# A hash attention and gated feed-forward kernel on one core: operand placement, a transfer's queue, the order of early loads, and the last output chunk

## The chip, the core and the metric

The kernel runs on one NeuronCore of a Trainium2 chip. The metric is the device time of one execution in microseconds (us); the figure given for a kernel is the median of its timed runs. Five engines work side by side, each on its own list of instructions in order: TensorE (PE in the profile, its weight loads PEld), VectorE (DVE), ScalarE (ACT), GpSimd (POOL) and SyncE (SP), which here only issues transfers. Transfers (DMAs) can be issued from SP's, ScalarE's or GpSimd's list; the issuing instruction first waits for what it needs, and holds up what is behind it on that list.

## The reference

The first part is attention in which a query sees only keys with the same hash. For each of 4 x 8 heads, with 768 positions of 64 values:

```python
q_bits = (np.einsum('bhsd,dk->bhsk', q, proj) > 0)      # 6 bits each; k_bits likewise
mask = q_bucket[:, :, :, None] == k_bucket[:, :, None, :]
scores = np.where(mask, scale * np.matmul(q, k.transpose(0, 1, 3, 2)), -1000000000.0)
attn = softmax(scores)                                   # over the keys
x = (attn @ v) rearranged to (3072 tokens, 512)
```

The second part is a gated feed-forward block with weights of 512 x 1536, 512 x 1536 and 1536 x 512, given in double precision:

```python
g = x @ w_gate;  silu = g / (1.0 + np.exp(-g))
out = (silu * (x @ w_val)) @ w_out                       # (3072, 512), float32
```

## The kernel before, in words

**Memory.** Tiles come from pools that are laid out in the order in which they are opened (L69 to L76): `wordp` (three buffers of 4096 bytes a partition, raw weight words), `stagep` (two of 12288 bytes, weights being prepared), `small` (three buffers each of the tiles `e`, 4 bytes, and `few`, 48 bytes), then `xparts_p`, `lastp`, the weight ring and the pools of the two parts.

**Attention.** The heads are taken two at a time: 16 pairs, each with two halves of 384 queries and six chunks of 128 keys, so 12 units a pair. For a pair:

- `front` prepares it. For pair 0, TensorE transposes q and k (`transpose`, L418, "tps") and `hash_own` (L455) multiplies by the projection ("hps"), takes signs on ScalarE (L441) and spreads them to the second head's rows with VectorE (`spread_k` L447, the copy at L463). The blocks are done one by one by `prepare_pair`, called before the units and within the first of them (L501, L614). For later pairs VectorE transposes k and q (L474), and `hash_next` (L465) does both hashes at once; here q's signs are copied to the second head's rows by a transfer, `spread_q` (L452, "qb<-qb"), which SP's list issues.
- `score(u)` (L494) multiplies k and q ("sc" from "qT,kT"), then adds the product of the sign rows ("sc" from "qb,kb"), which acts as the mask, and ScalarE takes exponentials into the tile `A` (L507). VectorE adds up the weights (L539, L543, L546).
- `attend(u)` (L510) multiplies the weights with v ("av").
- `total` (L551) and `invert` (L565) send the sums through small transfers on SP's list ("few<-row", "sums<-few", "r<-sums"), and `norm` divides.

The loop over pairs (L605) runs all 12 units' scores, then the hash of the next pair, then all 12 `attend`s. `load(n + 2, ...)` fetches later pairs on SP's list: q and k (eight transfers of 96 KB, L337) and v (L316). q and k have one buffer each, so their loads wait until the pair before has been transposed. At the start SP's list holds pair 0's loads, `load_words(2)` (two of 512 KB, L126), and then pair 1's q, k and v; GpSimd's list has the third words (L409 to L412).

**Weight pieces.** Between these steps (`begin_pieces`, `advance_pieces`, L170 to L184) ScalarE and VectorE turn the 36 weight pieces from double precision into three float32r parts (L135 to L164). GpSimd's list stores them to DRAM ("ram<-stage") and fetches the next words.

**The gated block.** The tokens come in three blocks of 1024. The x of a block is four tiles, one for each pair of heads, of 2 x 3 x 512 values: three parts, of which the first two are multiplied with the weights' first two parts ("a") and the third with the third ("n"); the difference corrects the rounding. `x_home` (L250) chooses the tile: block 0 has all four in `xparts_p`, block 1 its first two in `stagep`, and block 2 its last two in `stagep`. The matmuls are in `up` (L672): for a gate or value step, 16 of "a" and 8 of "n", with weights from a ring that GpSimd refills (L244). The down steps ("D" in `order`, "o" in the profile) take three hidden tiles at a time; the last of a block adds eight chunks of 128 tokens into the output tiles. In the very last step each chunk has nine matmuls into a tile of two PSUM banks: three of the correction, then six of the main product; `end` (L756) subtracts the one (L760), adds the other (L768), and SP's list stores the chunk (L775).

Of the kernel before, what the change touches and what calls it, by code (L numbers as in the profile page):

```python
# [13 lines left out]
ALU = mybir.AluOpType  # L14
# [5 lines left out]
def kernel(  # L20
# [20 lines left out]
    nc = tc.nc  # L41
# [25 lines left out]
    TOWARD = 1 - 2.0**-13  # L67

    konst = ctx.enter_context(tc.tile_pool(name="konst", bufs=1))  # L69
    wordp = ctx.enter_context(tc.tile_pool(name="wordp", bufs=3))  # L70
    stagep = ctx.enter_context(tc.tile_pool(name="stagep", bufs=2))
    small = ctx.enter_context(tc.tile_pool(name="small", bufs=3))
    xparts_p = ctx.enter_context(tc.tile_pool(name="xparts", bufs=1))
    lastp = ctx.enter_context(tc.tile_pool(name="lastp", bufs=1))
    RINGS = (3, 3)
# [43 lines left out]
    def load_words(count, queue=None):  # L119
        queue = queue or queues[0]  # L120
        for i in range(len(words), min(count, NPIECE)):
            words[i] = t = wordp.tile([P, PIECE, 2], I32, tag="words", name="words")
            to = t.rearrange("p f w -> p (f w)")
            if len(pieces[i].shape) == 3:
                to = to.rearrange("p (j c) -> p j c", j=NJ)
            queue.dma_start(to, pieces[i])  # L126
# [171 lines left out]
    def attention(scope):  # L298
# [13 lines left out]
        def fetch(n, name, queue, half=None):  # L312
            b, pr = pairs[n]
            if name == "v":
                t = raws["v", n] = raw.tile([P, 2, NCH, D], FP32, tag="vraw", name="vraw")
                queue.dma_start(  # L316
                    t.rearrange("p h c d -> p h (c d)"),
                    v[b, 2 * pr : 2 * pr + 2].rearrange("h (p c) d -> p h (c d)", c=NCH),
                )
                return  # L320
            src = q if name == "q" else k
            if not half:
                raws[name, n] = raw.tile([P, NCH, 2, D], FP32, tag=name + "raw", name=name + "raw",
                                         bufs=1)
            t = raws[name, n]
            if n == 0:
                cs = slice(None) if half is None else slice(half * CH, (half + 1) * CH)
                for h in range(2):
                    queue.dma_start(t[:, cs, h, :],
                                    src[b, 2 * pr + h].rearrange("(p c) d -> p c d", c=NCH)[:, cs, :])  # L330
                return
            blocks = t.rearrange("p c a b -> p (c a b)").rearrange(
                "p (c a d) -> p c a d", a=P // BLOCK, d=BLOCK)
            for h in range(2):
                for x in range(D // BLOCK):
                    at = h * D + x * BLOCK
                    queue.dma_start(  # L337
                        blocks[at : at + BLOCK],
                        src[b, 2 * pr + h][:, x * BLOCK : (x + 1) * BLOCK].rearrange(
                            "(a p c) d -> p c a d", c=NCH, p=BLOCK))  # L340
# [65 lines left out]
        for t in (sides["k", 0], sides["q", 0], sides["q", 1]):  # L406
            nc.gpsimd.memset(t, 0.0)

        load_words(2, nc.sync)  # L409
        for name, queue in (("q", nc.sync), ("k", nc.sync), ("v", nc.sync)):  # L410
            fetch(1, name, queue)
        load_words(3)  # L412

        T = {}
        bits = {}
# [1 line left out]
        def front(n):  # L417
            def transpose(name, half):  # L418
                if (name, n) not in T:
                    T[name, n] = opnd.tile([P, S], FP32, tag=name + "T", name=name + "T")  # L420
                ps = bank("tps")
                for i in range(CH):
                    nc.tensor.transpose(ps[:, i * P : (i + 1) * P],
                                        raws[name, n][:, half * CH + i, :, :].rearrange("p h d -> p (h d)"),
                                        ident)
                nc.scalar.activation(T[name, n][:, half * HQ : (half + 1) * HQ], ps[:, 0:HQ], AF.Copy,
                                     scale=2 / OFF if name == "k" else 1.0)

            bits["q", n] = sides["q", n % 2]
            bits["k", n] = sides["k", n % 2]  # L430
            low, high = slice(0, BLOCK), slice(D, D + BLOCK)

            def hash_blocks(todo):
                tile_ = bank("hps")
                for i, (name, half) in enumerate(todo):
                    nc.tensor.matmul(tile_[i * BLOCK : (i + 1) * BLOCK, 0:HQ], hash_w,  # L436
                                     T[name, n][:, half * HQ : (half + 1) * HQ],
                                     start=True, stop=True)

                def sign(i, name, half, to=low, **how):  # L440
                    nc.scalar.activation(bits[name, n][to, half * HQ : (half + 1) * HQ],  # L441
                                         tile_[i * BLOCK : (i + 1) * BLOCK, 0:HQ], AF.Sign,
                                         **(how or {"bias": nudge[name]}))

                return [lambda i=i, at=at, **how: sign(i, *at, **how) for i, at in enumerate(todo)]

            def spread_k(times, cols=slice(0, S)):  # L447
                b = bits["k", n][:, cols]
                for to, by in ((high, times[1]), (low, times[0])):
                    nc.vector.tensor_scalar(b[to], b[low], scalar1=by, scalar2=None, op0=ALU.mult)  # L450

            def spread_q():  # L452
                nc.sync.dma_start(bits["q", n][high], bits["q", n][low])

            def hash_own(*todo):  # L455
                for f in hash_blocks(todo):
                    f()
                for name, half in todo:
                    cols = slice(half * HQ, (half + 1) * HQ)
                    if name == "k":  # L460
                        spread_k(mask, cols)
                    else:
                        nc.vector.tensor_copy(bits["q", n][high, cols], bits["q", n][low, cols])  # L463

            def hash_next(todo):  # L465
                q0, q1, *ks = hash_blocks(todo)
                q0()
                q1()
                spread_q()
                return ks + [lambda: spread_k(times_k)]  # L470

            def transpose_blocks(name):
                T[name, n] = opnd.tile([P, S], FP32, tag=name + "T", name=name + "T")
                nc.vector.transpose(T[name, n], raws[name, n].rearrange("p c h d -> p (c h d)"))  # L474

            order = [("q", 0), ("q", 1), ("k", 0), ("k", 1)]
            if n:
                return [lambda name=name: transpose_blocks(name) for name in "kq"] + [
                    lambda: hash_next(order)]
            turns = [lambda x=x: transpose(*x) for x in order]  # L480
            return [turns[2], turns[0], lambda: hash_own(("k", 0)), lambda: hash_own(("q", 0)),
                    turns[3], turns[1], lambda: hash_own(("k", 1), ("q", 1))]

        units = [(n, half, c) for n in range(len(pairs)) for half in range(2) for c in range(NCH)]
        acc = {}
# [8 lines left out]
        def score(u):  # L494
            n, half, c = units[u]
            qs = slice(half * HQ, (half + 1) * HQ)
            ks = slice(c * P, (c + 1) * P)
            sc = [bank("sc")[:, 0:HQ] for _ in range(2)]
            for x, start in ((T, True), (bits, False)):
                if u < 2 and not start:  # L500
                    prepare_pair(1)  # L501
                for h in range(2):
                    rows = slice(h * D, (h + 1) * D)
                    nc.tensor.matmul(sc[h], x["k", n][rows, ks], x["q", n][rows, qs],  # L504
                                     start=start, stop=not start)
            for h in range(2):
                nc.scalar.activation(weights(u)[:, h, 0:HQ], sc[h], AF.Exp,  # L507
                                     scale=SCALE * (OFF / 2 if n == 0 else 1.0))
# [84 lines left out]
        def prepare_pair(count):  # L593
            for _ in range(count):
                if steps:
                    rest.extend(f for f in steps.pop(0)() or [] if f)
# [56 lines left out]
    def gated_block(scope):  # L653
# [7 lines left out]
        def two_banks(name):  # L661
            return pp.tile([P, 2, 512], FP32, tag="pp", name=name)
# [35 lines left out]
        def atoms_of(kind, n):  # L698
# [33 lines left out]
            else:  # L732
# [47 lines left out]
                ahead = 4 if part == NF // NQ - 1 else 0  # L780
                for c in range(ahead):
                    yield lambda c=c: start(c, range(NQ - 1))
                for c in range(NCB):
                    def chunk(c=c):
                        start(c, [NQ - 1] if c < ahead else range(NQ))
                        end(c)
                    yield chunk
# [96 lines left out]
```

## Time and profile before

| | |
|---|---|
| three timed runs | 923.06, 923.29, 925.82 us |
| median | 923.29 us |
| the profiled execution | 927.82 us |
| its span, first to last instruction | 926.0 us |
| granted TensorE clock, mean | 0.998 |
| TensorE busy | 912.7 us (99%) |
| VectorE, ScalarE, GpSimd busy | 666.4 (72%), 456.2 (49%), 91.6 us (10%) |

Attention takes the first third of the span, the gated block the rest. Matmuls are pipelined, so a busy TensorE row says only that nothing was missing there; how long a stretch of matmuls takes is read from their starts, in the chain of waits and in tables of stages. A line of a timeline gives the start, the duration, the engine, the line of the kernel, the operation, its output and inputs by the program's names, and how many there were; a bracket gives the idle time before it, and what ended it. A "q" behind an engine's name (SPq) means its list of issued transfers.

### The profile page before, as it was taken

Reading aid. Unit: us, or ns where it says so; the run is one execution under the profiler, and the core shown is the slowest. Engines: PE = TensorE matmul, PEld = TensorE weight load, DVE = VectorE, ACT = ScalarE, POOL = GpSimd, SP = SyncE. Lnnn points to the kernel's source line nnn. Section 1 sums busy time; section 2 is a strip of 40 time slices with the busy share of each in tenths; the row PEclk is TensorE's granted clock in tenths of the full one; section 3 lists DMA queues with packets and bytes.
Section 4 is the critical chain, followed back from the end, with each engine's and each line's share of the span. In section 5 each row is a group of like instructions: output and inputs, shape, how many; then the busy total and the mean of one; then the engine's idle time right before and its main releaser. Section 6 shows DMA issues by size and latency. Waiting matters only on the chain.

```text
span 926.0 us, 12980 instructions
## 1 busy us (share of the span) xinstructions
PE 912.7 (99%) x4789; PEld 638.9 (69%) x4789; DVE 666.4 (72%) x768; ACT 456.2 (49%) x814; POOL 91.6 (10%) x182
## 2 busy tenths in 40 slices
PE   8999989999999999999999999999999999999997
PEld 3444544444444478888888788888887888888886
DVE  4889989889989858779786756464658754474746
ACT  6889868888888654452414133331313233313220
POOL 2011100001101111000100000101010100001000
PEclk9999999999999999999999999999999999999999
DMA  7678787767886599685756563434444642526232
GB/s 171 136 185 205 201 207 172 166 180 200 242 213 206 179 384 318 229 284 206 292 187 243 207 226 103 175 133 170 137 145 151 234 147 103 187 69 208 99 136 92
DMA packets 145296, 174.28 MB, mean 188 GB/s; under 512 B 106481, under 2 KB 114897, under 8 KB 145233
## 3 DMA queue, kind: packets, MB, share of 16 engines
q0 software_dynamic: 22528, 116.14, 36.0%
q1 hardware_dynamic: 121904, 57.12, 24.3%
q8 instruction: 38, 0.62, 0.3%
q10 hardware_dynamic: 800, 0.20, 0.1%
q14 instruction: 26, 0.20, 0.1%
HBM read 133.17 MB, written 39.42 MB: 186 GB/s over the span
## 4 chain that ended last, share of the span: by engine, by line
PE 95%; DVE 2%; DMA 1%; SPq 1%; issue 0%; ACT 0%; DVEq 0%; ACTq 0%; POOLq 0%
PE a L670 29%; PE o L670 19%; PE sc L504 16%; PE n L670 14%; PE av L518 14%; PE sum L557 1%; PE hps L436 1%; SPq L337 1%; DMA kraw<-in_k_dram 0%; DVE hid L725 0%; DVE v L715 0%; DVE hid L723 0%; DVE v L719 0%; DMA qb<-qb 0%; DMA proj<-in_proj_dram 0%
## 5 line engine op out<-in xcount | busy, mean ns | idle before, releaser
L670 PE MATMUL a<-xparts,ring 128*128 128x512 f32 x1152 | 277.0, 392 | 0.6 <-ACT row L560 0.6
L670 PEld LDWEIGHTS a<-xparts,ring 128*128 128x128 f32 x1152 | 216.2, 188 | 50.2 <-ACT row L560 1.3
L670 PE MATMUL o<-ring,hid 128*128 128x512 f32 x864 | 198.7, 390 | 1.1 <-DVE hid L725 1.1
L670 PEld LDWEIGHTS o<-ring,hid 128*128 128x128 f32 x864 | 161.9, 188 | 36.0 <-DVE hid L725 2.4
L507 ACT ACTIVATE A<-sc 128x384 f32<-128x384 f32 x384 | 157.3, 492 | 12.6 <-PE sc L504 12.6
L504 PE MATMUL sc<-qT,kT 64*128 64x384 f32 x768 | 158.9, 491 | 0.0
L670 PE MATMUL n<-xparts,ring 128*128 128x512 f32 x576 | 144.3, 393 | 0.0
L518 PE MATMUL av<-A,vraw 128*64 128x386 f32 (+1 forms) x768 | 127.7, 488 | 0.0
L670 PEld LDWEIGHTS n<-xparts,ring 128*128 128x128 f32 x576 | 108.1, 188 | 24.3
L715 DVE TENSOR_TENSOR v<-v,n 128x1024 f32<-128x1024 f32 x36 | 44.0, 1221 | 104.0 <-PE n L670 103.4
L244 POOL DMA_DIRECT2D ring<-ram x108 | 56.9, 529 | 506.9 <-PE n L670 334.9
L504 PEld LDWEIGHTS sc<-qT,kT 64*128 64x128 f32 x768 | 69.2, 189 | 51.3 <-issue 50.3
L518 PEld LDWEIGHTS av<-A,vraw 128*64 128x64 f32 x768 | 53.7, 136 | 73.3 <-issue 61.6
L709 ACT ACTIVATE g<-a 128x1024 f32<-128x1024 f32 x36 | 37.0, 1026 | 134.0 <-PE a L670 127.8
L720 ACT ACTIVATE hid<-v 128x1024 fp32r<-128x1024 f32 x36 | 38.2, 1061 | 115.9 <-DVE v L719 112.9
L717 ACT ACTIVATE g<-g 128x1024 f32<-128x1024 f32 x36 | 38.2, 1061 | 84.7 <-DVE g L715 84.7
L772 DVE TENSOR_TENSOR o<-o 128x512 f32<-128x512 f32 x92 | 63.0, 687 | 20.6 <-ACT o L766 18.2
L504 PE MATMUL sc<-qb,kb 64*128 64x384 bf16 x384 | 65.4, 325 | 3.4 <-DMA qb<-qb 2.9
L715 DVE TENSOR_TENSOR g<-g,n 128x1024 f32<-128x1024 f32 x36 | 43.8, 1216 | 34.2 <-PE n L670 34.2
L539 DVE SCALAR_TENSOR_TENSOR both<-A 128x1536 f32<-128x1536 f32 x32 | 55.9, 1748 | 13.6 <-ACT A L507 13.0
L543 DVE TENSOR_TENSOR both<-both,A 128x1536 f32<-128x1536 f32 x32 | 56.3, 1759 | 3.3
L723 DVE SCALAR_TENSOR_TENSOR hid<-hid,v 128x1024 fp32r<-128x1024 f32 x36 | 44.0, 1223 | 19.2 <-ACT hid L720 19.1
(76 smaller groups left out, 696.9 us busy)
## 6 DMA issues: line engine op xcount, KB each, us to landing
ring<-ram POOLq DMA_DIRECT2D x108, 768.0 KB, 5.1
ram<-stage POOLq DMA_DIRECT2D x23, 768.0 KB, 5.7
ram<-stage SPq DMA_DIRECT2D x13, 768.0 KB
qraw<-in_q_dram SPq DMA_DIRECT2D x64, 96.0 KB
vraw<-in_v_dram SPq DMA_DIRECT2D x16, 384.0 KB
out_dram<-o SPq DMA_DIRECT2D x24, 256.0 KB
kraw<-in_k_dram SPq DMA_DIRECT2D x62, 96.0 KB
r<-sums SPq DMA_DIRECT2D x30, 192.0 KB
```

The source lines that it names most:

```text
L244: nc.gpsimd.dma_start(t.bitcast(FP32), ram[at].bitcast(FP32))
L504: nc.tensor.matmul(sc[h], x["k", n][rows, ks], x["q", n][rows, qs], start=start, stop=not start)
L507: nc.scalar.activation(weights(u)[:, h, 0:HQ], sc[h], AF.Exp, scale=SCALE * (OFF / 2 if n == 0 else 1.0))
L518: nc.tensor.matmul(ps[h * D : (h + 1) * D, 0:width], raws["v", n][:, h, c, :], a[:, h, 0:width], start=c == 0, stop=c == NCH - 1)
L539: nc.vector.scalar_tensor_tensor(out=t, in0=first, scalar=S * EPS / P / 2, in1=now, op0=ALU.add, op1=ALU.add)
L543: nc.vector.tensor_tensor(t, t, now, op=ALU.add)
L670: nc.tensor.matmul(ps, w, x, start=start, stop=stop)
L715: nc.vector.tensor_tensor(two(z), two(z), n_, op=ALU.subtract)
L717: nc.scalar.activation(z, z, AF.Silu)
L720: nc.scalar.activation(h, val, AF.Copy, scale=TOWARD / STEP)
L723: nc.vector.scalar_tensor_tensor(out=l, in0=h.bitcast(FP32), scalar=-STEP, in1=val, op0=ALU.mult, op1=ALU.add)
L772: nc.vector.tensor_tensor(accs[c], accs[c], t[:, 1], op=ALU.subtract)
```

## The change

It has five parts.

- The pool `small` is opened before `wordp` and `stagep`. The tiles and their sizes are the same.
- `spread_q`, the transfer of q's signs, is issued from GpSimd's list.
- At the start, `load_words(2)` ahead of pair 1's loads is gone; pair 1 is fetched in the order k, q, v; then SP's list loads all three first words.
- `hash_own` of pair 0's second halves is two steps, k and q, and `score` takes one step in unit 0 and two in unit 1.
- The very last chunk of the output is done by a function of its own: the correction goes into a separate tile, the main product is made in two halves of 256 columns, and each half is finished and stored by itself.

```diff
     konst = ctx.enter_context(tc.tile_pool(name="konst", bufs=1))
+    small = ctx.enter_context(tc.tile_pool(name="small", bufs=3))
     wordp = ctx.enter_context(tc.tile_pool(name="wordp", bufs=3))
     stagep = ctx.enter_context(tc.tile_pool(name="stagep", bufs=2))
-    small = ctx.enter_context(tc.tile_pool(name="small", bufs=3))
...
-        load_words(2, nc.sync)
-        for name, queue in (("q", nc.sync), ("k", nc.sync), ("v", nc.sync)):
-            fetch(1, name, queue)
-        load_words(3)
+        for name in "kqv":
+            fetch(1, name, nc.sync)
+        load_words(3, nc.sync)
...
-                nc.sync.dma_start(bits["q", n][high], bits["q", n][low])
+                nc.gpsimd.dma_start(bits["q", n][high], bits["q", n][low])
...
-                    turns[3], turns[1], lambda: hash_own(("k", 1), ("q", 1))]
+                    turns[3], turns[1], lambda: hash_own(("k", 1)), lambda: hash_own(("q", 1))]
...
-                    prepare_pair(1)
+                    prepare_pair(1 + u)
...
+                def last(c):
+                    t, tn = two_banks("o"), two_banks("o")
+                    cols = slice(c * P, (c + 1) * P)
+                    for j in range(NQ):
+                        mm(tn[:, 0], hs[j][:, 2, cols], ws[j][:, 2], j == 0, j == NQ - 1)
+                    nc.vector.tensor_tensor(accs[c], accs[c], tn[:, 0], op=ALU.subtract)
+                    batch, at = divmod(b * NCB + c, NCH)
+                    for half in range(2):
+                        here = slice(half * DM // 2, (half + 1) * DM // 2)
+                        for j in range(NQ):
+                            for v in range(2):
+                                mm(t[:, half, 0 : DM // 2], hs[j][:, v, cols], ws[j][:, v, here],
+                                   j == 0 and v == 0, j == NQ - 1 and v == 1)
+                        nc.vector.scalar_tensor_tensor(out=accs[c][:, here], in0=t[:, half, 0 : DM // 2],
+                                                       scalar=STEP + 1, in1=accs[c][:, here],
+                                                       op0=ALU.mult, op1=ALU.add)
+                        nc.sync.dma_start(rows[batch][:, at, here], accs[c][:, here])
+
                 for c in range(NCB):
+                    if final and c == NCB - 1:
+                        yield lambda: last(NCB - 1)
+                        return
```

## The prediction

> **What bounds the kernel now.** I read the page's chain of waits first: by engine it is almost all TensorE.
>
> ```profile
> PE 95%; DVE 2%; DMA 1%; SPq 1%; issue 0%; ACT 0%; DVEq 0%; ACTq 0%; POOLq 0%
> ```
>
> So a part of the change is worth only what it takes out of PE's own time, out of PE's waits, or out of the two ends. The second view is PE's own list of waits (us in total, times, longest):
>
> ```profile
> PE sc L504 <- DMA qb<-qb: 2.9, 1, 2.9
> PE hps L436 <- DVE qT L474: 1.9, 1, 1.9
> ...
> PE sc L504 <- DVE kb L450: 0.5, 1, 0.5
> ```
>
> These three are waits at places that the change touches. The third view is a table of stages: the pair whose scores hold the 2.9 us wait, and the next pair (columns: length, then busy time and count of PE, weight loads, VectorE, ScalarE, GpSimd, then granted clock, DMA share, GB/s):
>
> ```profile
> 119.50:143.61 24.11, 21.23 (x140) 11.24 (x137) 21.24 (x25) 16.30 (x38) 1.30 (x2) 0.93 0.81 165
> 143.61:162.84 19.23, 19.23 (x141) 9.20 (x137) 17.51 (x22) 16.07 (x38) 1.30 (x2) 1.00 0.72 174
> ```
>
> The wait costs 24.11 - 19.23 = 4.88 us, not 2.9: the clock is 0.93 in that pair, because the matmuls behind the gap run slower for a while. VectorE is busy 21.2 of 24.1 us, so it has little to spare. The fourth view is the same table for two gate or value steps (32 "a" and 16 "n" matmuls) in each block of 1024 tokens, counting only instructions on the x tiles:
>
> ```profile
> 331.19:342.06 10.87, 10.87 (x49) 9.00 (x49) 0.00 (x0) 0.00 (x0) 1.00 1.02 405
> 527.85:538.98 11.13, 11.13 (x50) 9.01 (x49) 0.00 (x0) 0.00 (x0) 1.00 1.03 411
> 727.39:738.52 11.13, 11.13 (x49) 9.01 (x49) 0.00 (x0) 0.00 (x0) 1.00 0.77 296
> ```
>
> PE is full in all three at clock 1.00, yet the same matmuls take 0.26 us longer in blocks 1 and 2. SP's queue around the first of these waits, from the timeline (start, us):
>
> ```profile
> 116.90 7.05 SPq L337 DMA_DIRECT2D qraw<-in_q_dram  x4
> 123.99 2.99 SPq L337 DMA_DIRECT2D kraw<-in_k_dram  x4
> 127.08 0.59 SPq L562 DMA_DIRECT2D few<-row  x1
> 127.77 0.59 SPq L453 DMA_DIRECT2D qb<-qb  x1
> ```
>
> ScalarE had finished q's signs at 120.80, but SP handed their copy over at 127.77, behind eight loads for a later pair.
>
> **One phase.** `wordp` (3 x 4096 bytes a partition) and `stagep` (2 x 12288) stand first, then `small`: three buffers of 4 bytes and three of 48. If each is rounded up to 32 bytes that is 3 x 32 + 3 x 64 = 288 = 4.5 x 64, so everything after `small` (x tiles, rings, hidden tiles) is 32 bytes off a multiple of 64, and `stagep` is not. Block 0 has all its x in the later pool; in blocks 1 and 2 two of the four x tiles live in `stagep` (L253 to L260). In the trace the 16 "a" matmuls of a step take 3.63 us in block 0 and 3.71 in blocks 1 and 2 (chain, block by block), the 8 "n" 1.81 and 1.85. That is 0.08 for eight matmuls on `stagep` tiles and 0.04 for four: the same 10 ns each, as if only those tiles were slow. The change puts `small` first, and all of them get the phase that block 0 already has. Saving: 0.26 us per two steps, 12 times in a block, in two blocks: 0.26 x 24 = 6.2; from the longer stretches of six steps between two down steps, 33.40 and 33.39 against 32.64 us, it is 0.76 x 4 x 2 = 6.0. I take 6.0. A rule of the Trainium skill speaks against this: SBUF — State Buffer, "Who interferes with whom", gives PE two independent read ports, one for the moving operand and one for weights, and says that PE never waits on anyone. By that rule two operands' relative place cannot matter, and the saving is 0. The row decides for me, since only the place of x differs between these stretches; but place could also mean something other than the phase, so 0 stays one end.
>
> **The signs' copy on GpSimd's queue.** It leaves SP, where it stood behind `load(n+2)`, whose buffers VectorE frees. On GpSimd it stands behind the weights' stores and loads of the stage before. For pair 6 GpSimd's last issue was at 115.70, 5.1 us before the signs were done; in the other pairs it was 3 us or more ahead. So it is issued about when the signs end. Need: the second head's first mask matmul comes 128.16 - 120.80 = 7.4 us after the signs (6.6 to 7.4 in all pairs). Landing: no 48 KB copy by GpSimd is shown; the small `proj` loads landed in 3.4 us, 768 KB stores in 5.7, 512 KB loads in 7 to 8; nearest in size is 3.4, plus about 0.6 for the issue. That fits. Here too a rule speaks against the move: the same page, "SBUF: two separate sides", says a GpSimd-issued DMA cannot get its descriptors written while VectorE holds the shared port in a two-port mode (its example grows from about 0.6 to 3.1 us). VectorE's copy-like L450 runs in just this window, but each of its two instructions takes 0.4 us and the long L539/L543 take 1.76; even with one of the latter, 0.6 + 3.4 + 1.8 = 5.8 us is under 6.6. By the row the wait goes, by the rule it also goes but with 0.8 us to spare. Saving in the profiled run: 4.88, and 0.22 in pair 5 (its pitch was 19.45 against 19.23): 5.1. What is late next is VectorE. In pair 6 its L450 ended at 127.47, 0.7 us before use; q's transposition for pair 6 ended 1.9 us before its hash. Without the gap, pair 7's hash falls at 118.74 + 19.23 = 137.97 and its transposition ended at 136.24, 1.7 us ahead; L450 of pair 7, less its waits for PE, has about 0.9. Thin, but not negative. GpSimd's fifteen added issues of 0.6 us lie in idle time (it is 10% busy).
>
> **The start.** Now q's loads for pair 1 are issued first (10.49, when q's last transposition frees the buffer), k's at 13.69; k's could start at 9.07. With k first, the eight issues (3.16 + 2.77 us here) run from 9.1 to about 15, and land some 3.7 us after the last, as k's did: near 18.7. The weights' words follow them; the first is used by ScalarE near 25, and 512 KB took 7 to 8 us from GpSimd, so issued at 15 to 17 they just arrive; a late one would delay ScalarE, which has slack behind "av", not PE. Hashing k's second half earlier (inside unit 1) takes the 0.55 us wait for L450 out of unit 3. But ScalarE then does its sign before unit 1's exponentials, so unit 3's start about 0.27 earlier only. VectorE's chain behind them (L539 1.76, L543 1.76, L546 0.96) sits directly in front of the transpositions, which now also lose their wait:
>
> ```profile
> 20.37 0.98 DVE L474 STREAM_TRANSPOSE kT<-kraw 128x768 f32<-128x768 f32 x1 [0.79 <-DMA kraw<-in_k_dram]
> ```
>
> 0.79 + 0.27 = 1.06 us. From above it is bounded by PE's two waits, 1.86 + 0.55 = 2.4; from below by the 0.27. I take 1.0.
>
> **The last chunk.** Now:
>
> ```profile
> 910.63 10.73 PE L670 MATMUL o<-ring,hid 128*128 128x512 f32 x46 [0.35 <-DVE hid L725]
> ...
> 920.08 0.69 DVE L768 SCALAR_TENSOR_TENSOR o<-o 128x512 f32<-128x512 f32 x1
> 921.39 0.69 DVE L760 TENSOR_TENSOR o<-o 128x512 f32<-128x512 f32 x1 [0.62 <-PE o L670]
> 922.12 0.69 DVE L768 SCALAR_TENSOR_TENSOR o<-o 128x512 f32<-128x512 f32 x1
> ```
>
> The nine last matmuls run 919.33 to 921.37. L760 reads only the bank that the first three filled, yet starts after the ninth: waits are for the whole two-bank tile. In the change the subtraction has a tile of its own, so it runs behind chunk 6, 920.8 to 921.5. Twelve half-wide matmuls: 0.113 us each (half of 0.227) to 0.188 (one weight load); nearest are the 128-wide transpositions at 0.109 with loads as wide, so I take 0.12. First half done by 921.0. VectorE on 256 columns, from 1.22 us for 1024 and 0.69 for 512: 0.42, so 921.5 to 921.9. If the second half's matmuls must wait for that read of the same tile, they end near 922.95 and the last step at 923.4, 0.6 later than now (922.81); if not, it ends at 922.4, 0.4 earlier. The transfer is half as large: the skill's DMA: Bandwidth & Descriptors, "Anatomy of one DMA", gives 2.0 us plus bytes over 436 GB/s, an estimated 0.3 less; no run shows it. So +0.3 or -0.7. L760 shows waits by whole tile: +0.3.
>
> **The sum.** The profiled execution took 927.82 (span 926.0 and 1.8 around it): 927.82 - 6.0 - 5.1 - 1.0 + 0.3 = 916.0. The median of three is 923.29, 4.5 lower than the profiled one. PE is back to back elsewhere, so a run can be 4.5 shorter only where PE waits for transfers, and the 4.88 us stall is the one large enough. I therefore take the timed runs as having only 5.1 - 4.5 = 0.6 of it: 923.29 - 6.0 - 0.6 - 1.0 + 0.3 = 916.0. Both ways meet.
>
> **Rivals.**
> - The timed runs hold the whole stall and the 4.5 is something that both kernels carry: 923.29 - 11.8 = 911.5. For it: the queue is late because VectorE frees buffers late, which repeats. Chance 0.18.
> - The phase is not the cause, or the tiles keep theirs: no 6.0, so 922.0, within what can be told from no change (0.3%, 2.8 us). For it: the rule on ports. Against: block 0. Chance 0.12.
> - VectorE becomes the bound in pairs 6 and 7, with 0.7 to 0.9 us to spare and GpSimd now sharing its port: some 1.5 us back, 917.5. Chance 0.10.
> - Slower: GpSimd's queue delivers the signs late. The place is the second head's mask matmul, L504, at each pair's start; it decides from a landing over 7.4 us after the signs (behind a 512 KB load of 7 to 8 us, or starved by VectorE). Each such pair costs 4.88 with the clock; pairs 5 to 7 would give 3 x 4.88 = 14.6: 916.0 + 14.6 = 930.6. Against: the loads are issued 5 us or more earlier. Chance 0.05.
>
> The forecast has 0.55. **Range:** 911.0 to 919.0 takes in the forecast, the full stall and VectorE as bound, with both ends of the tail and of the start: 0.83. Faster by over 0.3% (under 920.5): 0.85, the forecast, the full stall, VectorE as bound, and 0.02 of the second rival where it meets the full stall; within: the other 0.10; slower: 0.05.
>
> **What would show it.** Two steps in blocks 1 and 2 take 10.87, not 11.13. PE's waits hold no qb row, every pair from 2 to 14 is 19.23 long, and the clock stays 1.00. The first "av" starts near 22.1 instead of 23.14, with the transpositions following L546 at once. In the tail a gap of some 0.4 us stands on PE between the two halves. I am wrong if blocks 1 and 2 keep 11.13, if pair 6 shows a wait for VectorE, or if the qb copy lands over 6 us after its signs.

## The result, and the profile after

| | before | after |
|---|---|---|
| timed runs, side by side on one chip | 922.95 to 925.82 us | 915.87 to 916.18 us |
| median | 923.29 us | **915.88 us** |
| the profiled execution | 927.82 us | 915.88 us |
| its span | 926.05 us | 914.06 us |

The ratio is 0.9917, with a 95% interval of 0.9904 to 0.9930. The forecast was 916.0. The changed kernel's runs lie within 0.3 us of each other, those of before within 3, and its profiled execution is no longer above the median. A line of the code after stands up to four lines off the one before (L504 is now L503, L760 is L759, L768 is L767).

PE's own list of waits in the kernel after (us in total, times, longest):

```profile
PE idle L367 <- DVE kb L364: 1.3, 1, 1.3
PE o L669 <- DVE o L795: 1.2, 1, 1.2
PE o L669 <- DVE hid L724: 1.1, 3, 0.4
PE hps L435 <- ACT A L506: 1.0, 1, 1.0
```

The three waits shown of before are gone: no row names "qb", and none L449, the mask step that was L450. In place of the 1.9 us wait for q's transposition stands one of 1.0 us. The profile puts it down to ScalarE's exponentials (L506); `tiles_and_turn5` below shows that it is still for the transposition. One wait is new, for L795, in the last chunk. The table of stages for the same two pairs (length, then busy time of PE, weight loads, VectorE, ScalarE, GpSimd, then clock, DMA share, GB/s):

```profile
118.44:137.67 19.23, 19.23 (x140) 9.24 (x137) 18.10 (x22) 16.07 (x38) 1.85 (x3) 1.00 0.80 186
137.67:156.90 19.23, 19.23 (x140) 9.20 (x137) 18.43 (x23) 16.06 (x38) 1.85 (x3) 1.00 0.76 188
```

24.11 has become 19.23, PE is never idle, and the clock stays at 1.00; VectorE is busy for 18.4 of 19.2 us. Two gate or value steps in each block, the x tiles alone:

```profile
325.06:335.94 10.88, 10.88 (x49) 9.02 (x48) 0.00 (x0) 0.00 (x0) 1.00 1.00 391
521.56:532.44 10.88, 10.88 (x49) 9.01 (x48) 0.00 (x0) 0.00 (x0) 1.00 1.04 411
718.06:728.94 10.88, 10.88 (x49) 9.02 (x48) 0.00 (x0) 0.00 (x0) 1.00 0.81 307
```

All three blocks now run at block 0's pace. The signs' copy, asked for by its tile (duration of the issue in ns, first and last start, then the time to landing):

```profile
L452 POOL DMA_DIRECT2D qb<-qb x15: 513/522/529, 24.3 to 293.1; - x15
...
DMA to landing us min/median/max: 1.8/2.5/5.3
```

GpSimd issues it 0.3 us after the signs end (0.6 in pair 1). The slowest, pair 6's, lands 5.6 us after its signs, where 7.4 us were there to spend. The landings differ: the five copies that were issued while a 512 KB load of weights from the same list was still under way (pairs 4 to 8) took 3.0 to 5.3 us, the other ten 1.8 to 2.6. The start, from the timeline:

```profile
9.10 2.83 SPq L337 DMA_DIRECT2D kraw<-in_k_dram  x4
...
12.04 2.69 SPq L337 DMA_DIRECT2D qraw<-in_q_dram  x4
...
18.66 0.96 DVE L545 TENSOR_TENSOR acc<-both 128x768 f32<-128x768 f32 x1
19.54 0.97 DVE L473 STREAM_TRANSPOSE kT<-kraw 128x768 f32<-128x768 f32 x1
20.43 0.93 DVE L473 STREAM_TRANSPOSE qT<-qraw 128x768 f32<-128x768 f32 x1
21.51 0.52 PE L435 MATMUL hps<-qT,hash 128*32 128x384 f32 x2 [0.98 <-ACT A L506]
```

VectorE's list runs from the sums straight into the transpositions; the wait of 0.79 us for k is gone. The tail, from the timeline:

```profile
907.28 0.69 DVE L759 TENSOR_TENSOR o<-o 128x512 f32<-128x512 f32 x1 [0.16 <-PE o L669]
908.00 0.69 DVE L767 SCALAR_TENSOR_TENSOR o<-o 128x512 f32<-128x512 f32 x1
908.61 0.68 DVE L787 TENSOR_TENSOR o<-o 128x512 f32<-128x512 f32 x1
909.39 0.42 DVE L795 SCALAR_TENSOR_TENSOR o<-o 128x256 f32<-128x256 f32 x1
...
909.87 0.98 PE L669 MATMUL o<-ring,hid 128*128 128x256 f32 x6 [1.24 <-DVE o L795]
910.89 0.42 DVE L795 SCALAR_TENSOR_TENSOR o<-o 128x256 f32<-128x256 f32 x1 [1.07 <-PE o L669]
```

PE stands for 1.24 us between the halves, until VectorE has read the first one out of the same tile.

The 11.99 us between the two spans, cut at marks that both traces have:

| stretch | before | after | difference | forecast |
|---|---|---|---|---|
| to the first "av" | 23.13 | 22.29 | -0.84 | -1.0 |
| pairs 5 and 6 | 19.45 + 24.11 | 19.23 + 19.23 | -5.10 | -5.1 |
| first "a" to the subtraction of chunk 6 | 593.93 | 587.79 | -6.14 | -6.0 |
| from there to the end | 6.69 | 6.78 | +0.09 | +0.3 |

### The profile page after: what moved, and what is told of

It is laid out like the page before. It is cut to its first block, busy times and chain, and to the rows that moved or that the text cites. A ratio compares the mean times of both kernels' runs of the same rounds, so it can differ in the third digit from the quotient of the medians.

```text
span 914.1 us, 12999 instructions
## 1 busy us (share of the span) xinstructions
PE 904.9 (99%) x4795; PEld 636.9 (70%) x4795; DVE 665.5 (73%) x769; ACT 455.8 (50%) x814; POOL 99.1 (11%) x196
## 4 chain that ended last, share of the span: by engine, by line
PE 96%; DVE 2%; ACT 1%; issue 0%; DVEq 0%; ACTq 0%
PE a L669 29%; PE o L669 19%; PE sc L503 17%; PE n L669 14%; PE av L517 14%; PE hps L435 1%; PE sum L556 1%; ACT A L506 1%; DVE hid L724 0%; DVE hid L722 0%; DVE v L714 0%; DVE v L718 0%; PE idle L367 0%; DVE xparts L292 0%; PE tps L422 0%
## 5 line engine op out<-in xcount | busy, mean ns | idle before, releaser
L669 PE MATMUL a<-xparts,ring 128*128 128x512 f32 x1152 | 273.0, 390 | 0.6 <-ACT row L559 0.6
L669 PE MATMUL o<-ring,hid 128*128 128x512 f32 (+1 forms) x870 | 199.0, 389 | 2.3 <-DVE o L795 1.2
L506 ACT ACTIVATE A<-sc 128x384 f32<-128x384 f32 x384 | 157.0, 492 | 7.6 <-PE sc L503 7.6
L503 PE MATMUL sc<-qT,kT 64*128 64x384 f32 x768 | 156.9, 487 | 0.0
L669 PE MATMUL n<-xparts,ring 128*128 128x512 f32 x576 | 142.3, 390 | 0.0
L503 PEld LDWEIGHTS sc<-qT,kT 64*128 64x128 f32 x768 | 67.5, 187 | 48.5 <-issue 47.9
L503 PE MATMUL sc<-qb,kb 64*128 64x384 bf16 x384 | 63.3, 323 | 0.0
L722 DVE SCALAR_TENSOR_TENSOR hid<-hid,v 128x1024 fp32r<-128x1024 f32 x36 | 44.0, 1223 | 19.2 <-ACT hid L719 19.1
```

What stands on the lines that cost most here:

```text
L669: nc.tensor.matmul(ps, w, x, start=start, stop=stop)
L722: nc.vector.scalar_tensor_tensor(out=l, in0=h.bitcast(FP32), scalar=-STEP, in1=val, op0=ALU.mult, op1=ALU.add)
```

## The experiments

The theory is the forecast's: phase 6.0, start 1.0, tail +0.3, and the copy's stall, which the median of before hardly holds. Rivals: the whole 4.9 us is in the timed runs too; the phase is not the cause; VectorE becomes the bound.

**One part alone.** Four kernels are the one before with one part of the change each.

`small_first`, the pool moved:

```diff
+    small = ctx.enter_context(tc.tile_pool(name="small", bufs=3))
     wordp = ctx.enter_context(tc.tile_pool(name="wordp", bufs=3))
     stagep = ctx.enter_context(tc.tile_pool(name="stagep", bufs=2))
-    small = ctx.enter_context(tc.tile_pool(name="small", bufs=3))
```

> Only the pool order: small is opened before wordp and stagep; all else as before. Theory (a matmul is about 10 ns longer when its x tile and its weights lie at different 32-byte phases): blocks 1 and 2 take 5.44 us for 16 + 8 matmuls, as block 0 does, and the time falls by 6.0 to about 917.3 us. Rival (it is the stage pool's region, or what else runs in blocks 1 and 2, that is slow): those blocks stay at 5.56 us and the time at 923.3.

Measured: 917.69 us, ratio 0.9926 (0.9904 to 0.9949). Two steps, by block:

```profile
326.15:337.03 10.88, 10.88 (x49) 9.01 (x48) 0.00 (x0) 0.00 (x0) 1.00 1.00 399
522.65:533.53 10.88, 10.88 (x49) 9.01 (x48) 0.00 (x0) 0.00 (x0) 1.00 1.03 411
719.15:730.03 10.88, 10.88 (x49) 9.01 (x48) 0.00 (x0) 0.00 (x0) 1.00 0.80 309
```

One line moved gives block 0's pace everywhere, and most of the gain. The ratio flatters it a little: 14 of the 29 runs of before in this set had a mean clock under 0.999. Against the other 15 (median 923.68 us), at the clock that all six runs here had, the gain is 6.0 us.

`copy_on_gpsimd`, the copy alone:

```diff
-                nc.sync.dma_start(bits["q", n][high], bits["q", n][low])
+                nc.gpsimd.dma_start(bits["q", n][high], bits["q", n][low])
```

> Only the copy of q's signs is moved to GpSimd's list. In the profile both theories expect no PE wait for qb and 19.23 us for the pair that took 24.11. They differ on the timed runs. Theory (the timed runs of before mostly lack the 4.9 us stall of its profiled run): the median falls by 0.6 to about 922.7, and the spread of the runs above it goes. Rival (the timed runs hold the whole stall): the median falls by 5.1 to about 918.2.

Measured: 923.48 us, ratio 0.9987 (0.9973 to 1.0001), so 1.2 us with an interval from 2.5 to nothing. Among the runs at a mean clock of 0.999 or more (eight of twelve here, 15 of before) the medians are 923.16 and 923.68 us, 0.5 apart, near the 0.6 expected. The whole stall in the timed runs (918.2) is out. PE's waits in its profile:

```profile
PE hps L436 <- DVE qT L474: 2.2, 1, 2.2
PE idle L367 <- DVE kb L364: 1.3, 1, 1.3
PE o L670 <- DVE hid L725: 1.1, 3, 0.4
PE sc L504 <- DVE kb L450: 0.8, 2, 0.5
```

"qb" is gone. VectorE's L450 holds PE for 0.8 us: 0.5 of it stands at the start, as in the kernel before, and 0.3 is new, in pair 6. The table for pairs 1 and 6:

```profile
23.93:44.61 20.68, 20.68 (x139) 9.61 (x136) 15.59 (x18) 15.81 (x36) 2.08 (x3) 0.93 0.79 149
121.58:141.27 19.69, 19.40 (x140) 9.43 (x136) 18.34 (x22) 16.08 (x38) 1.86 (x3) 1.00 0.84 180
```

The second line is the rival VectorE, real and small: 19.69 - 19.23 = 0.46 us, of which PE was idle for 0.29. The first has no idle PE at all and is still 1.45 longer than 19.23: the clock was low behind the wait at the start.

`loads_reordered`, the order at the start, without the split hash:

```diff
-        load_words(2, nc.sync)
-        for name, queue in (("q", nc.sync), ("k", nc.sync), ("v", nc.sync)):
-            fetch(1, name, queue)
-        load_words(3)
+        for name in "kqv":
+            fetch(1, name, nc.sync)
+        load_words(3, nc.sync)
```

> Only the order of the first loads: pair 1's k, q, v ahead of the three words, all on SP's list; the hash of pair 0's second halves stays one step. Theory (VectorE's 0.79 us wait for k is the whole gain at the start, and splitting the hash gives nothing): the first av starts near 22.3 instead of 23.14, the median falls by 0.8 to about 922.5. Rival (the split is needed too, or the words now arrive late): av near 22.9 or later, the median within 0.3 of before.

Measured: 924.36 us, ratio 0.9995 (0.9978 to 1.0013): a miss in the median. Six runs took 922.1 to 922.8 us at a mean clock of 0.999 or more, as expected, and six 925.9 to 926.7 at 0.997 to 0.998. Its own stretch is plain in its timeline:

```profile
9.11 2.84 SPq L337 DMA_DIRECT2D kraw<-in_k_dram  x4
...
19.51 0.97 DVE L473 STREAM_TRANSPOSE kT<-kraw 128x768 f32<-128x768 f32 x1
...
22.27 1.19 PE L517 MATMUL av<-A,vraw 128*64 128x386 f32 x6
```

The first "av" comes at 22.27, with the split hash at 22.29. In these profiles the split gives nothing.

`last_halves`, the last chunk alone:

```diff
+                def last(c):
+                    t, tn = two_banks("o"), two_banks("o")
...
+                    if final and c == NCB - 1:
+                        yield lambda: last(NCB - 1)
+                        return
```

> Only the last chunk in two halves. Theory (the second half's matmuls wait for VectorE's read of the first half because both lie in one tile; the smaller transfer gives back 0.45): last VectorE step 0.58 later, the end 0.1 later, 923.4. Rival (the halves overlap as written and the tail gains): 922.6.

Measured: 923.44 us, ratio 1.0001 (0.9979 to 1.0023). Nothing that can be told from no change, as forecast. PE's list of waits has the new one already:

```profile
PE o L670 <- DVE o L796: 1.2, 1, 1.2
```

**The phase, taken apart.** `ring_off_32` is the kernel after with an unused tile of 32 bytes ahead of the ring (filled with zeros once, and read by nothing), so that x and weights part again while x tiles stay together:

```diff
+    padp = ctx.enter_context(tc.tile_pool(name="padp", bufs=1))
+    pad = padp.tile([P, 8], FP32, tag="pad", name="pad")
...
+        nc.gpsimd.memset(pad, 0.0)
```

> The changed kernel with an unused 32-byte tile ahead of the weight ring: x tiles stay 32 bytes off a multiple of 64, ring, hidden tiles and everything behind lie on it. Theory (two different phases of weights and moving x cost about 10.4 ns a matmul): all 1728 matmuls on x are slow, 5.44 becomes about 5.68 us for 16 + 8 in all three blocks, the down steps (ring and hidden tiles together) stay at 16.32 us for 72, and the time is 915.9 + 18.0 = 933.9 us. Rival (a moving operand on a multiple of 64 is slow by itself): x stays fast, 5.44, and the down steps, whose moving operand is the ring, become slow: 864 x 10.4 ns = 9.0, 924.9 us.

Measured: 928.0 us, ratio 1.0038 (1.0023 to 1.0053), slower than before. Two steps of block 0, and from the chain of waits a down step:

```profile
325.49:336.69 11.20, 11.20 (x49) 9.02 (x48) 0.00 (x0) 0.00 (x0) 1.00 1.01 396
...
364.85 16.32 PE o L672 x72
```

All three blocks are slow, and the "o" steps, whose hidden tiles move with the ring, are not (16.32 to 16.35 us for 72, and 16.32 in the kernel after). So the rule is about the distance between weights and moving operand. But the price is 0.32 / 48 = 6.7 ns a matmul, not the 10.4 expected.

`all_at_64` is the kernel before with that tile behind `small`, so that `stagep` and the ring are 288 + 32 = 320 bytes apart, a multiple of 64:

```diff
     small = ctx.enter_context(tc.tile_pool(name="small", bufs=3))
+    padp = ctx.enter_context(tc.tile_pool(name="padp", bufs=1))
+    pad = padp.tile([P, 8], FP32, tag="pad", name="pad")
...
+        nc.gpsimd.memset(pad, 0.0)
```

> The kernel before with an unused 32-byte tile behind small: the pools keep their order, and all of them start at multiples of 64. Theory (only a difference of phases costs): all blocks at 5.44 us, the median 6 to 7 us under before, as with small opened first. Rival (a multiple of 64 is slow by itself): all blocks at about 5.68, and 12 us slower than before.

Measured: 925.07 us, ratio 1.0003 (0.9987 to 1.0019). Blocks 0 and 1:

```profile
328.88:339.76 10.88, 10.88 (x49) 9.01 (x48) 0.00 (x0) 0.00 (x0) 1.00 1.00 395
525.53:536.62 11.09, 11.09 (x49) 9.00 (x48) 0.00 (x0) 0.00 (x0) 1.00 1.03 411
```

The theory fell: 320 bytes apart, though a multiple of 64, is slow as well. Block 0 is fast here at another place than in the kernel before, so it isn't x's own place that counts. Two more kernels, each run once, are `ring_off_128` and `ring_off_256`, with the tile of `ring_off_32` made 128 and 256 bytes long:

```diff
-    pad = padp.tile([P, 8], FP32, tag="pad", name="pad")
+    pad = padp.tile([P, 32], FP32, tag="pad", name="pad")
```

```diff
-    pad = padp.tile([P, 8], FP32, tag="pad", name="pad")
+    pad = padp.tile([P, 64], FP32, tag="pad", name="pad")
```

> The changed kernel with an unused tile of 128 bytes ahead of the weight ring, so that ring and x tiles are 128 bytes apart in place of 0, both still 32 bytes off a multiple of 64. What is open after the last call: a distance of 64 bytes was slow too. If the distance counts to a period of 128 bytes, 16 + 8 matmuls take 5.44 us in all blocks; if the period is longer (256 or 512; weight tiles 512 bytes apart behave alike), they take about 5.60.

> The same with an unused tile of 256 bytes. Period 128 or 256: 5.44 us. Period 512: about 5.60.

Measured: 927.42 and 916.02 us. Block 1 of each:

```profile
525.50:536.70 11.20, 11.20 (x49) 9.01 (x48) 0.00 (x0) 0.00 (x0) 1.00 1.03 411
```

```profile
521.66:532.54 10.88, 10.88 (x49) 9.01 (x48) 0.00 (x0) 0.00 (x0) 1.00 1.03 410
```

0 and 256 bytes are fast; 32, 128 and 288 are slow, and so is 320. All other pools between them are whole multiples of 256 long, and `small` does take 288: in the program of the kernel before `stagep` starts at byte 28800 of a partition and the ring at 105888, which is 301 x 256 + 32 further on. So the distance counts modulo 256 bytes. Other remainders than 0, 32, 64 and 128 were not tried.

**What the new waits are worth.** `three_tiles` is the kernel after with a PSUM tile for each half:

```diff
-                    t, tn = two_banks("o"), two_banks("o")
+                    tn, *t = [two_banks("o") for _ in range(3)]
...
-                                mm(t[:, half, 0 : DM // 2], hs[j][:, v, cols], ws[j][:, v, here],
+                                mm(t[half][:, 0, 0 : DM // 2], hs[j][:, v, cols], ws[j][:, v, here],
```

> The changed kernel, the two halves of the last chunk in tiles of their own. Theory (the wait of 1.2 us on PE between the halves is for VectorE's read of the same tile): no wait there, the second half's step follows the first on VectorE at once, the last step ends 1.0 us earlier, 914.9 us. Rival (the wait is for something else, such as the free tile): 915.9.

Measured: 915.44 us, ratio to before 0.9906 (0.9884 to 0.9927). The wait for L795 is gone; its tail:

```profile
907.56 0.69 DVE L759 TENSOR_TENSOR o<-o 128x512 f32<-128x512 f32 x1 [0.17 <-PE o L669]
...
908.89 0.68 DVE L787 TENSOR_TENSOR o<-o 128x512 f32<-128x512 f32 x1
909.68 0.76 DVE L795 SCALAR_TENSOR_TENSOR o<-o 128x256 f32<-128x256 f32 x2
```

The last step ends at 910.44, 2.88 us after its mark, instead of 4.03. From the first "a" to the end its profile is 0.97 us shorter than that of the kernel after. Its first "av" came 0.26 us later, so the profiled executions differ by 0.72; the medians, measured on two chips, differ by 0.44.

`tiles_and_turn5` has the same and an earlier place for pair 1's transpositions, ahead of VectorE's last long sum:

```diff
-        TURN = 8
+        TURN = 5
```

> As the kernel with three tiles, and pair 1's transpositions (and the loads of pair 2) are put at unit 5 instead of unit 8 of pair 0, ahead of VectorE's second addition. Theory (PE's gap of 1.0 us before pair 1's hash is VectorE's order, since k and q have landed by then): the gap goes, the first av at about 21.3 instead of 22.3, 913.9 us. Rival (the data have not landed, or the additions now hold up another step): 914.9 or more.

Measured: 913.83 us, ratio 0.9890 (0.9868 to 0.9911), the best version of all. Its start:

```profile
14.10 7.33 ACT L506 ACTIVATE A<-sc 128x384 f32<-128x384 f32 x18 [0.33 <-PE sc L503]
...
16.68 0.97 DVE L473 STREAM_TRANSPOSE kT<-kraw 128x768 f32<-128x768 f32 x1
...
18.44 1.72 DVE L542 TENSOR_TENSOR both<-both,A 128x1536 f32<-128x1536 f32 x1
...
20.46 0.52 PE L435 MATMUL hps<-qT,hash 128*32 128x384 f32 x2
...
21.25 1.19 PE L517 MATMUL av<-A,vraw 128*64 128x386 f32 x6
```

The first "av" is another 1.04 us earlier than in the kernel after, 22.29 - 21.25. The hash starts at 20.46, although ScalarE's exponentials run to 21.43, as they do in the kernel after. So the hash does not need them, and the 1.0 us in the kernel after was for q's transposition, which ended there at 21.36, 0.15 us before the hash. In the profiled run pair 6 took 19.84 us for 19.23, and PE's list of waits names VectorE's mask step:

```profile
PE sc L503 <- DVE kb L449: 0.4, 1, 0.4
```

`turn5_less_pieces` is `tiles_and_turn5` and tries to take that away, by moving a weight piece from pair 3 to pair 7:

```diff
-        PACE = [2] * 4 + [1] * 4 + [2, 1] * 4
+        PACE = [2] * 3 + [1] * 4 + [2] + [2, 1] * 4
```

> As the kernel with three tiles and the transpositions at unit 5, with one weight piece less in pair 3 and one more in pair 7. Theory (pair 6 lost 0.6 us there to VectorE's mask step L449, late from the piece work of pairs 3 to 5): pair 6 is 19.23 us long again and the time is 0.6 lower, 913.2. Rival (its lateness has another source, or the piece is missed in pairs 7 to 9): 913.8 or more, with a wait in another pair.

Measured: 914.05 us, ratio 0.9890 (0.9873 to 0.9907). Pair 6 is 19.23 in its profile, but the median isn't lower: a miss. The 0.6 us was in that one execution, the slowest of four.

**Why the copy was late.** `loads_behind_copy` is the kernel before, with the copy still on SP's list and the loads of q and k behind it:

```diff
-                if i == (2 if n else TURN):
-                    load(n + 2, "qk")
...
+            load(n + 2, "qk")
```

> The kernel before with the copy of q's signs still on SP's list, and the loads of pair n + 2's q and k issued behind it in place of ahead. Theory (the place behind those eight loads makes the copy late, not SP's list): no PE wait for qb, pairs 5 and 6 near 19.23 us, and no run with the clock dip of the stall; the gap at the start stays. Rival (SP's transfers are late by themselves, or the loads now come too late for VectorE): PE still waits for qb, or its hash waits for the transposition, and some pairs are over 20 us.

Measured: 923.03 us, ratio 0.9992 (0.9977 to 1.0007), no wait for "qb", and all 14 stretches from one pair's first "av" to the next are 19.23. One of the ten runs took 926.31 us at a mean clock of 0.998, where none was expected; the profile is of another run and does not show why. SP's list in the timeline:

```profile
120.52 0.59 SPq L453 DMA_DIRECT2D qb<-qb  x1
121.20 2.76 SPq L337 DMA_DIRECT2D qraw<-in_q_dram  x4
```

The copy is issued at 120.52, seven us sooner than in the kernel before. SP's list was not too slow for it; the place behind loads that wait for buffers was. For the median that is worth no more than the move to GpSimd.

## Why the prediction was right, and where it was not

**The phase: right in size, its period wrong.** The forecast was 6.0 (the second of its two sums, 0.76 x 4 x 2, is 6.1 and not 6.0); the stretch gave 6.14, and the edit alone gave 6.0 at an equal clock. "32 bytes off a multiple of 64" was the step that failed: the period is 256 bytes, as 128 and 320 show, and the edit worked because it took the distance to a multiple of 256. That the wrong period pointed to an edit that works was luck; the same reason called for 6 to 7 us from `all_at_64`, which gave none. "The same 10 ns each, as if only those tiles were slow" held as a sum and not as a price. With every matmul off it is 6.7 ns. Where slow tiles alternate with matched ones it is 0.255 / 24 = 10.6, since in the trace of before matched matmuls right behind slow ones are longer too, by 1 to 9 ns. From the Trainium skill's rule (SBUF — State Buffer, "Who interferes with whom") that PE's two read ports are independent and that PE waits on no one, the prediction worked out a saving of 0 as the other end. It did not come out: relative place cost 0.32 us in 10.88. Whether it is the two reads that meet, no trace shows.

**The stall: the right number, for a rougher reason.** The profile gave back 5.10 of 5.1, and the median 0.5 to 1.2 by `copy_on_gpsimd`, near the 0.6 taken. But the timed runs are not alike in holding "0.6 of it". In the sets of the experiments, the kernel before ran 65 times: 40 runs at a mean clock of 0.999 or more with a median of 923.4 us, and 25 below it with 926.3. Four profiles are of the longer kind, and each shows what sets it apart: a clock halved for some us, at pair 6's wait in the kernel before and in `last_halves`, and behind the wait at the start in `copy_on_gpsimd` and `all_at_64`. The timed runs themselves give only the mean clock. In `loads_reordered`, with the start's wait shortened, six of twelve were of the longer kind. Of the kernel after and the six built on it, none of 29 was. `small_first`, which touches neither wait, had none in six either, but `all_at_64`, which touches neither as well, had nine of twelve, so the six may be chance. So a part of the gain that one median hides is that the long runs are gone.

**The sum.** That 916.0 met 915.88 so closely is luck in part: the start gave 0.16 less than forecast, the phase 0.14 more, and the tail cost 0.21 less. Of the 7.41 us between the medians these three stretches of the profiles make 6.89, which leaves 0.5 for the stall, where 0.6 was taken.

**The copy on GpSimd.** Its issue was as forecast. Its landing was 2.5 us in the median, under the 4.0 taken, but 4.9 and 5.3 in pairs 5 and 6, over it and under the 5.8 feared. A copy behind a 512 KB load was among the rivals, and was set aside because the loads are issued 5 us or more earlier. In the kernel after, pair 6's load was issued 4.7 us ahead of the copy and landed 2.4 us after the copy's issue. The rule against the move did not decide: VectorE was busy for 94 and 96% of the two stretches shown, and the copies in them took 5.3 and 3.4 us. No run separates the load from VectorE's port. In `tiles_and_turn5` pair 6's copy landed 6.5 us after its signs, past the 6 us that the prediction named as a sign of being wrong, and still 1.5 us before its matmul.

**The start.** 0.84 came of 1.0: the 0.79 of VectorE's wait for k did, the 0.27 of earlier exponentials did not. The hash of both second halves side by side had taken PE 0.77 us; split, each step takes 0.76 alone, and unit 3's exponentials start at 14.10 as against 14.06. The step counted what the split moves forward and not that it gives up the pairing.

**The tail.** +0.09 for +0.3. The last VectorE step came 4.03 us after the mark, 0.58 later, as worked out (0.6); the end behind it was 0.5 shorter, not the estimated 0.3; the section cited for that estimate gives its formula for transfers that GpSimd issues, and SP issues these. The wait by whole tile is shown by `three_tiles`. The "0.4 us" announced for PE's gap contradicted the prediction's own times, which give 0.9; it was 1.24, since the half-wide matmuls (0.12 us each, as taken) were done by 908.63 and VectorE came to them only at 909.39.

**VectorE as the bound** was rated at 0.10. In the kernel after its mask step ends 0.65, 0.40 and 1.12 us ahead of its use in pairs 5, 6 and 7, where 0.9 was worked out for pair 7. It did cost 0.46 us in `copy_on_gpsimd`'s profile and 0.61 in that of `tiles_and_turn5`.

## What to carry to other kernels

Keep the start of the weights and the start of the moving operand a multiple of 256 bytes apart in float32r matmuls such as these: one odd little pool between large ones cost 6 us here. A small transfer that is needed soon goes ahead of loads that wait for buffers, or on another list. Halves of a result overlap only in tiles of their own, and before a stall in one profile is believed, the spread and the clocks of the timed runs should agree with it.

## What the runs showed of the hardware

- A float32r matmul of 128 x 512 goes at 0.2267 us (10.88 / 48) when the distance between its operands' starts is a multiple of 256 bytes, and at 0.2333 (11.20 / 48) when it is 32 or 128 more.
- A wait of PE of 2 to 3 us can halve the clock, and need not. In the kernel before, the 2.88 us wait for "qb" was followed by 3.4 us at 0.50; in `all_at_64` a wait of 2.0 us at the start was, too; in `last_halves` one of 2.4 us at the start was not:

```profile
131.40:134.80 3.40, 3.40 (x14) 2.21 (x15) 3.30 (x6) 1.36 (x3) 0.53 (x1) 0.50 0.54 122
...
24.29:27.70 3.41, 3.41 (x14) 1.41 (x12) 3.24 (x4) 3.35 (x7) 0.00 (x0) 0.50 0.83 130
...
20.00:26.00 6.00, 3.62 (x30) 1.25 (x25) 4.99 (x4) 3.49 (x8) 0.00 (x0) 1.00 0.29 51
```

  In `copy_on_gpsimd`, a wait of 2.2 us at the start did it. In `last_halves` the clock was at 0.50 for 6.8 us around pair 6's wait of 2.6. The Trainium skill (TensorE: Matmul & The Clock Gate, "What's actually happening") puts it at an idle window of some 3.4 us whose phase runs free. The 3.4 us at half clock and the chance from run to run agree with that, the idle time doesn't: these waits were shorter. The kernel after, with no wait over 1.3 us in its profile, showed a clock of 0.999 or more in all five runs.
- A copy of 48 KB within SBUF, issued by GpSimd, landed in 1.8 to 5.3 us, median 2.5; in 1.8 to 2.6 when no 512 KB load of the same list was under way.
